# Routed rows sent in half sequences, each scatter tied to a VectorE step, five read-back slots

## The chip, the cores and the metric

One core of a Trainium2 chip runs the whole program. The metric is the time of one execution on the device, in microseconds; the median of three runs stands for a kernel. One further execution was profiled, and every row below is from it.

## What is computed

Four sequences of 11456 tokens with 128 features go through a long convolution and then, token by token, through a mixture of eight experts with top-1 routing:

```python
h_filt = (relu(pos_emb @ w1) @ w2) * exp(-0.01 * pos)[:, None]
y = irfft(rfft(x * v, n=2*S, axis=1) * rfft(h_filt, n=2*S, axis=0), axis=1)[:, :S]
x = (x * y).reshape(B * S, D)                       # B, S, D = 4, 11456, 128
logits = x @ w_gate + modality_bias[modality_id]    # 8 experts
e_idx = argmax(logits, axis=1); gate_w = softmax(logits)[e_idx]
for e in range(8):                                  # F = 1024
    out[e_idx == e] = gate_w * (relu(x @ w1[e]) @ w2[e])
```

All inputs are float32; out has 45824 rows of 128.

## The kernel before, in words

**The convolution** is written as transforms of size 90 by 64. For each sequence b there are two kinds of stage. `outer` number b works in 16 steps: it takes sequence b-1 through its inverse transform and its routing, and sequence b through its forward transform (`outer` 4 has only the first part, `outer` 1 to 3 have both). `middle` b works in 23 groups: it multiplies spectra. The order is filter, `middle` 0, `outer` 1, `middle` 1, `outer` 2, `middle` 2, `outer` 3, `middle` 3, `outer` 4, experts. A `Timeline` sorts all parts by step and by a place within the step; the engines (TensorE, VectorE, ScalarE and the SyncE queue) then keep that order. SyncE issues nearly all loads and stores, from one queue, in program order. GpSimd issues the indirect transfers.

**Routing.** Every two steps of an `outer` give one block o of 0 to 7: `choice(o)` picks an expert for 1440 rows, `store(o)` writes the rows (130 words each, with gate weight and token number) to a DRAM buffer `xr[b]`, `send(o)` counts places within each expert's region, `places(o)` writes them to `xi[b]`. When the sequence is complete, `fetch(b)`, called in group 4 of the next `middle`, loads the places (`to`). The rows come back to SBUF in pieces (`rows_back`): 128 partitions by 5 rows, in three slots, each asked for three columns before it is needed. A column is 128 rows, one to a partition, and one indirect transfer of GpSimd, here called a scatter, sends it to its places in `xs`. A sequence has 90 columns, all four have 360.

**Where scatters are issued.** `send_rows(n, behind, wait)` takes the next n columns. In `middle` it is called once a group after group 4, in GpSimd's order but without a wait for another engine. In `outer` it is called through `paced`, which makes the scatter wait for the VectorE instruction just given: two for the products of the forward transform (lines 469 and 473), one each for line 695 and line 697 of the inverse transform (three and two in `outer` 4), one for line 788 of `choice` (not for the last sequence). GpSimd's queue is in order, and a scatter also waits for the eighth before it.

**The experts** work on 82 tiles of 512 rows and up to 22 of 256. A full tile has eight steps c; each step is one block of the hidden layer (three matmuls, ScalarE's relu at line 1065, VectorE's rest at line 1066) and three matmuls of the second layer for a block two steps back. At c = 2 `rows_out` turns the tile before back (lines 1097, 1099) and issues its four output scatters at once (line 1102). The rows of the last sequence are fetched at step 18 and sent at five steps of nine, with no wait for another engine:

```python
if lo == 0 and at == FC:
    fetch(nb - 1)
if lo == 0 and 5 * at % 9 < 5:
    send_rows(1)
```

Tiles of the first 37 need the rows of the first two sequences alone (180 scatters). `rest()` makes the tables of the later tiles, one VectorE instruction a step from tile 28 (`FR = 9`).

Of the kernel before, what the change touches and what calls it, by code (L numbers as in the profile page):

```python
# [31 lines left out]
N1, N2 = 90, 64  # L32
# [38 lines left out]
FR = 9  # L71
# [20 lines left out]
def shape_constants():  # L92
# [48 lines left out]
        "c_fwd": f(fwd.reshape(D, 2 * N1)), "c_whole": f(whole.reshape(D, 2 * N1)),  # L141
        "c_inv": f(inv.reshape(N1, D)), "c_to": f(to), "c_back": f(back), "c_win": f(win.reshape(D, 2 * N2)),
# [36 lines left out]
def hyena_moe_kernel(ctx: ExitStack, tc: tile.TileContext, a: dict, out: bass.AP,  # L179
# [8 lines left out]
    NR = 4 * HALF * N2  # L188
    xr = [dram.tile([NR, RW], F32, name=f"xr{b}") for b in range(nb)]
    xi = [dram.tile([NR], I32, name=f"xi{b}") for b in range(nb)]  # L190
# [26 lines left out]
    to_t = [cst.tile([D, NR // D], I32, name=f"to{i}") for i in range(2)]  # L217
    RC = 5
    NB = NR // D // RC
    back_t = [cst.tile([D, RC, RW], F32, name=f"back{i}") for i in range(3)]  # L220
# [36 lines left out]
    def send_rows(n, behind=None, wait=None):  # L257


        for _ in range(min(n, len(waiting))):  # L260
            b, c = waiting.pop(0)
            if c % RC == 2:
                rows_back(b, c // RC + 1)
            ix, src = to_t[b % 2][:, c:c + 1], back_t[(b * NB + c // RC) % 3][:, c % RC]
# [92 lines left out]
    with ExitStack() as cv:  # L357
# [5 lines left out]
        def pair(name):  # L363
# [7 lines left out]
        win = bs2[:, 0].rearrange("p e c -> p (e c)")[:, 0:2 * N2].rearrange(  # L371
            "p (q m) -> p q m", q=NQ)
        whole = bs2[:, 2:4].rearrange("p o e c -> p (o e c)")[:, 0:2 * N1]
        wf = keepp.tile([D, 2, D], F32, name="wf")
        dve.memset(wf, 0.0)
# [41 lines left out]
        for name, of in (  # L417
                ("r", [t.rearrange("p c r -> p (c r)")[:, 0:U // 2] for t in back_t]),
                ("h0", [flat(t)[:, 0:2 * U] for t in xo_t]),
                ("seq0", [flat(t)[:, k * U:k * U + U] for t in xo_t for k in range(2)]  # L420
                 + [work[:, i * U:i * U + U] for i in range(4)])):
            ring_of[name] = [of, 0]
# [107 lines left out]
        def middle_stages(b):  # L530
# [76 lines left out]
            def spectrum(g):  # L607
# [59 lines left out]
        def inverse_stages(b):  # L667
# [57 lines left out]
        def route_stages(b):  # L725
# [36 lines left out]
            def choice(o):  # L762
# [27 lines left out]
                if b < nb - 1:  # L790
                    paced(s)

            def store(o):
                xo = xo_of(b, o)
                for blk in range(2):
                    rows = xr[b].rearrange("(k n w m) r -> k n w m r", k=2, n=HALF, w=2)
                    sp.dma_start(
                        rows[blk, :, :, 8 * o:8 * o + 8].rearrange("n w m r -> n w (m r)"),
                        xo[64 * blk:64 * blk + HALF].rearrange("p w s h r -> p w (s h r)"))

            def send(o):
# [13 lines left out]
                dve.tensor_mul(ro, ro, oh[0:PU])  # L815
# [6 lines left out]
            def places(o):  # L822
                ix = ix_t[(b * NO + o) % 2]
                for blk in range(2):
                    at = xi[b].rearrange("(k n w m) -> k n w m", k=2, n=HALF, w=2)
                    sp.dma_start(
                        at[blk, :, :, 8 * o:8 * o + 8],
                        ix[64 * blk:64 * blk + HALF].rearrange("p (w m) -> p w m", w=2))
# [57 lines left out]
        for b in range(nb + 1):  # L886
            if b:
                outer(b, at)
            if b < nb:
# [7 lines left out]
            if b == NK:  # L897
                line.put(at - 3, lambda: (dve.tensor_copy(base1, base),
                                          known.append(NK * NR // D)), 3)
# [73 lines left out]
    def experts(lo, hi):  # L973
# [4 lines left out]
        def rows_in(i):  # L978
# [11 lines left out]
            if tb == "1":  # L990

                for s in scatters[known[0]:]:
# [57 lines left out]
        def hidden(at):  # L1050
# [15 lines left out]
            dve.scalar_tensor_tensor(hl, ph, 0.0, hh.bitcast(F32), op0=ALU.max, op1=ALU.subtract)  # L1066
# [23 lines left out]
        def rows_out(i):  # L1090
# [21 lines left out]
        for at in range(len(work) + 6):  # L1112
# [19 lines left out]
            if c == 2:  # L1132
                rows_out(i - 1)

# [11 lines left out]
_INS = ["w1", "w2", "moe_w_gate", "moe_modality_bias",  # L1146
# [3 lines left out]
def device_inputs(inputs):  # L1150
# [3 lines left out]
    for name, of, lay in (("x", "x", tile4), ("xd", "x", tile8), ("v", "v", tile8)):  # L1154
# [9 lines left out]
        for a in ids])).view(np.int32).reshape(B, D, NO * NC, 2)  # L1164
    arrays.update(shape_constants())
# [18 lines left out]
```

## Time and profile before

| | us |
|---|---|
| median of 3 runs | 2283.65 (2272.26 to 2286.53) |
| the profiled execution's own time | 2303.19 |
| its span, first to last instruction | 2301.0 |
| TensorE busy in the span | 2118.4 (92%) |
| VectorE, ScalarE, GpSimd busy | 1753.4, 1317.3, 968.2 |

A matmul's end is modelled, so a busy TensorE is not one at its peak, and what a stretch costs is better read from the spacing of equal steps than from the busy share. "issue" as the releaser of a wait is time for which the profile shows no cause, "remote" an update whose sender it doesn't know. An idle engine matters only where the end waits for it.

### The profile page before, as it was taken

What the parts mean: (1) busy time and instruction counts of PE and PEld (TensorE: products, weight loads), DVE (VectorE), ACT (ScalarE), POOL (GpSimd) and SP (SyncE); (2) the same over time, 40 slices, a digit from 0 to 9 for tenths busy, and PEclk for the clock granted to TensorE, in tenths of its full rate; (3) what the DMA queues carried; (4) which work ended last, traced back from release to release, by engine and by line L of the source; (5) the groups of instructions that cost most, each with busy time, mean ns of one, the idle gap of its engine ahead of it and who ended that gap; (6) DMA issues with size and microseconds to landing.
All of it is one profiled execution on the core that took longest, in us unless ns stands there. A gap on an engine that the chain in (4) does not pass through costs nothing.

```text
span 2301.0 us, 48463 instructions
## 1 busy us (share of the span) xinstructions
PE 2118.4 (92%) x18002; PEld 1658.4 (72%) x18002; DVE 1753.4 (76%) x2790; ACT 1317.3 (57%) x2451; POOL 968.2 (42%) x910
## 2 busy tenths in 40 slices
PE   8999998989799888987788889999999999999997
PEld 7787665766477556744466667788888888888897
DVE  6677899978799779955465566778777777777796
ACT  4555674556445654444455455666666666666675
POOL 0233004855476555755234566533333333333332
PEclk9999999999899999988799899999999999999999
DMA  9354677888688887745567222111111111111110
GB/s 369 128 159 152 238 266 233 259 288 278 208 267 272 274 268 250 244 137 158 140 190 227 73 76 86 62 61 56 46 46 45 42 47 47 47 46 46 34 44 30
DMA packets 187833, 341.52 MB, mean 148 GB/s; under 512 B 31633, under 2 KB 99213, under 8 KB 187593
## 3 DMA queue, kind: packets, MB, share of 16 engines
q1 hardware_dynamic: 164137, 290.68, 39.7%
q0 software_dynamic: 23296, 47.66, 6.1%
q8 instruction: 144, 2.36, 0.4%
q14 instruction: 96, 0.79, 0.1%
q10 hardware_dynamic: 160, 0.03, 0.0%
HBM read 253.84 MB, written 84.83 MB: 147 GB/s over the span
## 4 chain that ended last, share of the span: by engine, by line
issue 41%; PE 33%; POOL 13%; DVE 6%; ACT 3%; DMA 2%; another core or an unknown queue 1%; SPq 0%; POOLq 0%; DVEq 0%; ACTq 0%
POOL out L1102 9%; PE pw L657 8%; PE pz L615 6%; PE py L690 5%; PE wt L681 4%; POOL xs L265 4%; PE s L484 3%; PE xT L738 2%; DVE work L631 1%; ACT A L487 1%; PE s L517 1%; PE pl L746 1%; PE pz L568 1%; PE pq L582 1%
## 5 line engine op out<-in xcount | busy, mean ns | idle before, releaser
L1066 DVE SCALAR_TENSOR_TENSOR hl<-ph,hh 128x512 fp32r<-128x512 f32 x724 | 497.6, 689 | 275.4 <-ACT hh L1065 167.0
L1065 ACT ACTIVATE hh<-ph 128x512 fp32r<-128x512 f32 x724 | 433.0, 600 | 412.0 <-PE ph L1062 257.3
L1102 POOL DMA_INDIRECT out<-ot,idx x362 | 355.9, 983 | 685.2 <-DVE ot L1099 600.7
L265 POOL DMA_INDIRECT xs<-back,to x360 | 388.0, 1078 | 249.9 <-issue 79.3
L1083 PE MATMUL po<-hh,wh 128*128 128x512 f32 (+1 forms) x792 | 306.4, 387 | 13.3 <-ACT hh L1065 6.7
L1060 PE MATMUL ph<-xh,wh 128*128 128x512 f32 (+1 forms) x792 | 306.7, 387 | 2.8 <-ACT wh L1031 2.2
L1085 PE MATMUL po<-hl,wh 128*128 128x512 f32 (+1 forms) x792 | 298.0, 376 | 0.1
L1062 PE MATMUL ph<-xl,wh 128*128 128x512 f32 (+1 forms) x792 | 297.8, 376 | 0.0
L1061 PE MATMUL ph<-xh,wl 128*128 128x512 f32 (+1 forms) x792 | 296.8, 375 | 0.0
L1084 PE MATMUL po<-hh,wl 128*128 128x512 f32 (+1 forms) x792 | 296.2, 374 | 0.0
L625 POOL TENSOR_TENSOR work<-work 128x512 f32<-128x512 f32 (+1 forms) x92 | 115.4, 1254 | 281.5 <-DVE work L621 281.4
L661 ACT COPY A<-pw 128x512 f32<-128x512 f32 (+1 forms) x184 | 97.0, 580 | 182.8 <-PE pw L657 182.8
L615 PE MATMUL pz<-A,work 128*64 128x256 f32 x1440 | 180.6, 393 | 6.2 <-DMA work<-in_c_to 5.7
L681 PEld LDWEIGHTS wt<-ident,A 128*90 128x90 f32 x1024 | 126.0, 185 | 79.5 <-issue 50.6
L657 PEld LDWEIGHTS pw<-work 64*128 64x128 f32 x2856 | 165.1, 188 | 25.1 <-ACT work L597 11.9
L1083 PEld LDWEIGHTS po<-hh,wh 128*128 128x128 f32 x792 | 150.5, 190 | 39.8 <-ACT hh L1065 8.6
L657 PE MATMUL pw<-work 64*128 64x128 f32 x2856 | 177.2, 277 | 0.0
L681 PE MATMUL wt<-ident,A 128*90 128x128 f32 x1024 | 148.8, 297 | 30.7 <-issue 21.6
L1085 PEld LDWEIGHTS po<-hl,wh 128*128 128x128 f32 x792 | 150.2, 190 | 32.2 <-DVE hl L1066 3.6
L1062 PEld LDWEIGHTS ph<-xl,wh 128*128 128x128 f32 x792 | 150.5, 190 | 28.2 <-DVE xl L1047 0.4
L1060 PEld LDWEIGHTS ph<-xh,wh 128*128 128x128 f32 x792 | 150.9, 191 | 26.7 <-ACT wh L1031 2.6
L682 ACT COPY work<-wt 90x512 f32<-90x512 f32 x256 | 136.7, 597 | 57.4 <-PE wt L681 25.5
(181 smaller groups left out, 3769.6 us busy)
## 6 DMA issues: line engine op xcount, KB each, us to landing
work<-hs SPq DMA_DIRECT2D x66, 512.0 KB
work<-in_x SPq DMA_DIRECT2D x64, 512.0 KB
work<-in_xd SPq DMA_DIRECT2D x54, 512.0 KB
work<-in_v SPq DMA_DIRECT2D x54, 512.0 KB
xr<-xo SPq DMA_DIRECT2D x64, 365.6 KB
back<-xr SPq DMA_DIRECT2D x72, 325.0 KB
work<-in_c_to SPq DMA_DIRECT2D x88, 256.0 KB
x<-xs SPq DMA_DIRECT2D x82, 260.0 KB
```

Source lines behind the costliest of these rows:

```text
L265: s = pool.indirect_dma_start(out=xs, out_offset=bass.IndirectOffsetOnAxis(ap=ix, axis=0), in_=src, in_offset=None, bounds_check=E * R - 1 ...
L615: pe.matmul(z[64 * s:64 * s + 64, t, r], k["b"][:, t, s, r], A[:, :, 4 * g + 2 * t + s], start=True, stop=True)
L657: pe.matmul(v[s][:, t, blk], k[of][at, t, r, blk], k["c"][at, t, r], start=i == 0, stop=i == len(terms) - 1)
L681: pe.transpose(p[0:N1, D * j:D * j + D], A[:, blk, :, 8 * q + 2 * j + c], ident)
L1060: pe.matmul(p, k[0, "h"][:, f:f + D], k["xh"], start=True, stop=False)
L1061: pe.matmul(p, k[0, "l"][:, f:f + D], k["xh"], start=False, stop=False)
L1062: pe.matmul(p, k[0, "h"][:, f:f + D], k["xl"], start=False, stop=True)
L1065: act.activation(hh, ph, AF.Relu)
L1066: dve.scalar_tensor_tensor(hl, ph, 0.0, hh.bitcast(F32), op0=ALU.max, op1=ALU.subtract)
L1083: pe.matmul(po, k[1, "h"][:, f], hh[:, t], start=g == 0, stop=False)
L1085: pe.matmul(po, k[1, "h"][:, f], hl[:, t], start=False, stop=g == NCH - 1)
L1102: s = pool.indirect_dma_start(out=out, out_offset=bass.IndirectOffsetOnAxis(ap=k["idx"][:, j:j + 1], axis=0), in_=ot[:, j, :], in_offset=N ...
```

## The change

1. `xr` and `xi` are now one buffer for each half sequence u (0 to 7, 45 columns); four `to` tiles in place of two.
2. Pieces are 3 rows to a partition in five slots (before: 5 in three), the same SBUF. `rows_back` is called ahead of every column and asks until the piece in use and two more are asked for.
3. The first half of a sequence is fetched in step 13 of its own `outer`, the second half in group 4 of the next `middle` (the last one at step 18 of the experts).
4. In `middle` one column is sent in every group. In `outer` line 697 no longer sends (it still does in `outer` 4), line 695 sends two in place of three in `outer` 4, `choice` sends in every sequence, and line 815 of `send(o)` sends one.
5. In the experts, `rows_out` only puts its four columns on a list. `pace` issues one a step at c = 3 to 6, tied to the step's line 1066, and a routed column at c = 7, 0 and 1, tied likewise. `rest()` starts at tile 32, two instructions a step.
6. At the start, `w1` and `w2` come as one array `wf` laid out by the host, by SyncE's first DMA; two tables come as one (`early`), by ScalarE's queue, ahead of its table load. GpSimd issues none of them.

```diff
-FR = 9
+FR = 5
...
-    NR = 4 * HALF * N2
-    xr = [dram.tile([NR, RW], F32, name=f"xr{b}") for b in range(nb)]
+    NR = 2 * HALF * N2
+    xr = [dram.tile([NR, RW], F32, name=f"xr{u}") for u in range(2 * nb)]
...
-    RC = 5
+    RC, NBACK = 3, 5
...
-    def rows_back(b, k):
-        if k < NB:
-            of = xr[b].rearrange("(p k c) r -> p k c r", p=D, c=RC)
-            sp.dma_start(back_t[(b * NB + k) % 3], of[:, k])
-    def fetch(b):
-        sp.dma_start(to_t[b % 2], xi[b].rearrange("(p c) -> p c", p=D))
-        rows_back(b, 0)
-        waiting.extend((b, c) for c in range(NR // D))
+    def rows_back():
+        now = waiting[0][1] // RC if waiting else len(ready)
+        while len(asked) < min(now + 3, len(ready)):
+            u, k = ready[len(asked)]
+            of = xr[u].rearrange("(p k c) r -> p k c r", p=D, c=RC)
+            sp.dma_start(back_t[len(asked) % NBACK], of[:, k])
+            asked.append((u, k))
+    def fetch(u):
+        sp.dma_start(to_t[u % 4], xi[u].rearrange("(p c) -> p c", p=D))
+        waiting.extend((u, u * NR // D + c) for c in range(NR // D))
+        ready.extend((u, k) for k in range(NB))
+        rows_back()
...
         for _ in range(min(n, len(waiting))):
-            b, c = waiting.pop(0)
-            if c % RC == 2:
-                rows_back(b, c // RC + 1)
+            rows_back()
+            u, c = waiting.pop(0)
...
         def first_constants():
+            sp.dma_start(wf, a["wf"].rearrange("p (a d) -> p a d", a=2))
+            act.dma_start(early, a["c_early"])
+            act.dma_start(fwd, a["c_fwd"].rearrange("p (c m) -> p c m", c=2))
             act.copy(warm[:, 1:2], warm[:, 0:1])
-            for j in range(2):
-                half = slice(64 * j, 64 * j + 64)
-                act.dma_start(wf[half, 1, half], a["w1"])
-            for j in range(2):
-                pool.dma_start(wf[64 * j:64 * j + 64, 0], a["w2"])
-            pool.dma_start(win, a["c_win"].rearrange("p (q m) -> p q m", q=NQ))
-            pool.dma_start(whole, a["c_whole"])
-            pool.dma_start(fwd, a["c_fwd"].rearrange("p (c m) -> p c m", c=2))
...
                 if g == GD + 2 and b > 0:
-                    fetch(b - 1)
-                if g > GD + 2:
-                    send_rows(1, s)
+                    fetch(2 * b - 1)
+                send_rows(1, s)
...
-                n = 2 if b == nb - 1 else 1
-                paced(dve.tensor_add(y[:, 0:512], py[:, 0], y[:, 512:1024]), 2 * n - 1)
+                paced(dve.tensor_add(y[:, 0:512], py[:, 0], y[:, 512:1024]), 1 + (b == nb - 1))
                 dve.tensor_sub(y[:, 512:1024], py[:, 0], y[:, 512:1024])
-                paced(dve.tensor_mul(xo_of(b, q // 2)[:, :, q % 2, :, 0:D], four(y),
-                                     four(kept.pop(q))), n)
+                s = dve.tensor_mul(xo_of(b, q // 2)[:, :, q % 2, :, 0:D], four(y),
+                                   four(kept.pop(q)))
+                if b == nb - 1:
+                    paced(s)
...
-                if b < nb - 1:
-                    paced(s)
+                paced(s)
...
-                dve.tensor_mul(ro, ro, oh[0:PU])
+                paced(dve.tensor_mul(ro, ro, oh[0:PU]))
...
             if b:
                 outer(b, at)
+                line.put(at + 13, lambda b=b: fetch(2 * b - 2), 3)
...
-            for j in range(n // D):
-                s = pool.indirect_dma_start(
-                    out=out, out_offset=bass.IndirectOffsetOnAxis(ap=k["idx"][:, j:j + 1], axis=0),
-                    in_=ot[:, j, :], in_offset=None, bounds_check=N - 1, oob_is_err=False)
-                free_rows(outs, s)
+            held.extend((k["idx"][:, j:j + 1], ot[:, j, :]) for j in range(n // D))
+
+        held, steps = [], []
+
+        def rows_away(wait=None):
+            ix, src = held.pop(0)
+            s = pool.indirect_dma_start(
+                out=out, out_offset=bass.IndirectOffsetOnAxis(ap=ix, axis=0),
+                in_=src, in_offset=None, bounds_check=N - 1, oob_is_err=False)
+            free_rows(outs, s)
+            if wait is not None:
+                tc.add_manual_dep(ins_of(s), wait.name, sync_dep, reason="pace")
+
+        def pace(i, c):
+            if held and c > 2:
+                rows_away(steps[-1])
+            elif lo == 0 and c in (7, 0, 1):
+                send_rows(1, wait=steps[-1])
...
             if lo == 0 and at == FC:
-                fetch(nb - 1)
-            if lo == 0 and 5 * at % 9 < 5:
-                send_rows(1)
+                fetch(2 * nb - 1)
+            if at < len(work):
+                pace(i, c)
             if NW1 - FR <= i < NW1:
+                next(others, 0)
                 next(others, 0)
```

The lists `ready` and `asked` hold the pieces that may be read and that have been asked for; `steps` holds every line 1066. `rows_out` of a 256-row tile, and of the last full one, issues what is left on the list at once, as before.

## Rows read from the trace of the kernel before

**Rows 1.** The page, slices of the span: GpSimd's busy tenths and TensorE's granted clock.
```profile
POOL 0233004855476555755234566533333333333332
PEclk9999999999899999988799899999999999999999
```

**Rows 2.** Windows (`outer` 1, `outer` 4, experts early and later): busy time and instructions by engine.
```profile
core 0: us, PE busy (x) PEld busy (x) DVE busy (x) ACT busy (x) POOL busy (x), PEclk, DMA share, GB/s
241.00:353.00 112.00, 106.15 (x1570) 72.13 (x1572) 103.17 (x194) 80.66 (x151) 0.00 (x0) 1.00 0.72 246
984.00:1136.00 152.00, 119.52 (x596) 70.75 (x595) 71.98 (x165) 64.00 (x122) 75.75 (x72) 0.78 0.49 136
1148.00:1479.00 331.00, 291.00 (x1284) 229.54 (x1284) 211.74 (x367) 176.99 (x324) 176.89 (x178) 0.95 0.39 125
1479.00:1800.00 321.00, 321.00 (x1517) 265.11 (x1517) 251.51 (x457) 207.98 (x380) 106.92 (x109) 1.00 0.16 50
```

**Rows 3.** Line 690 in `outer` 1 to 4: count, durations in ns, first and last start.
```profile
L690 PE MATMUL py<-work,inv x128: 592/592/832, 241.6 to 349.1; 90*64 90x512 f32 x128
L690 PE MATMUL py<-work,inv x128: 592/592/1116, 470.6 to 608.0; 90*64 90x512 f32 x128
L690 PE MATMUL py<-work,inv x128: 591/592/644, 731.4 to 862.3; 90*64 90x512 f32 x128
L690 PE MATMUL py<-work,inv x128: 592/643/1116, 984.6 to 1132.0; 90*64 90x512 f32 x128
```

**Rows 4.** Line 615 in `middle` 1 and 3, likewise.
```profile
L615 PE MATMUL pz<-A,work x360: 379/379/687, 357.8 to 461.5; 128*64 128x256 f32 x180
...
L615 PE MATMUL pz<-A,work x360: 379/379/687, 871.7 to 975.5; 128*64 128x256 f32 x180
```

**Rows 5.** Line 265, the routed scatters, around `outer` 2, in `outer` 4 and the experts.
```profile
L265 POOL DMA_INDIRECT xs<-back,to x69: 972/980/1972, 470.0 to 612.7; - x69
...
L265 POOL DMA_INDIRECT xs<-back,to x72: 977/980/1989, 988.6 to 1128.9; - x72
...
L265 POOL DMA_INDIRECT xs<-back,to x90: 977/980/1482, 1184.5 to 1469.4; - x90
```

**Rows 6.** Line 1065, one a step, in four windows of the experts.
```profile
L1065 ACT ACTIVATE hh<-ph x23: 585/598/622, 1147.9 to 1182.7; 128x512 fp32r<-128x512 f32 x23
L1065 ACT ACTIVATE hh<-ph x184: 585/598/622, 1147.9 to 1477.9; 128x512 fp32r<-128x512 f32 x184
L1065 ACT ACTIVATE hh<-ph x64: 597/598/610, 1361.6 to 1466.0; 128x512 fp32r<-128x512 f32 x64
L1065 ACT ACTIVATE hh<-ph x217: 597/598/615, 1479.3 to 1799.4; 128x512 fp32r<-128x512 f32 x109
```

**Rows 7.** GpSimd's timeline: ends of an early run, start of a later one.
```profile
1240.92 0.98 POOL L1102 DMA_INDIRECT out<-ot,idx  x1 [6.88 <-DVE ot L1099]
...
1258.90 0.98 POOL L265 DMA_INDIRECT xs<-back,to  x1 [0.30 <-issue]
...
1508.63 0.98 POOL L1102 DMA_INDIRECT out<-ot,idx  x1 [7.04 <-DVE ot L1099]
```

**Rows 8.** Waits: TensorE's loads in 1240 to 1262, ScalarE in 982 to 1140.
```profile
PEld pt L1097 <- issue: 6.6, 1, 6.6
...
ACT work L682 <- remote: 17.3, 8, 3.8
ACT work L748 <- remote: 9.0, 2, 5.1
ACT work L740 <- remote: 4.9, 4, 2.3
```

**Rows 9.** Waits: SyncE's queue for a read-back slot, GpSimd for rows.
```profile
SPq L249 <- DMA xs<-back,to: 26.8, 12, 6.0
...
POOL xs L265 <- DMA xr<-xo: 5.9, 2, 2.9
```

**Rows 10.** Timeline of the start: first loads and first matmuls.
```profile
0.76 0.88 SPq L498 DMA_DIRECT2D work<-in_pos_emb  x2
...
2.37 1.12 POOL L385 DMA_DIRECT2D wf<-in_w  x2
...
7.81 5.46 PE L504 MATMUL m<-wf,work 128*128 128x128 f32 x24 [7.81 <-DMA wf<-in_w]
```

More of the change, by code (lines that the diff above doesn't have):

```diff
@@ L140, in shape_constants @@
     return {
-        "c_fwd": f(fwd.reshape(D, 2 * N1)), "c_whole": f(whole.reshape(D, 2 * N1)),
-        "c_inv": f(inv.reshape(N1, D)), "c_to": f(to), "c_back": f(back), "c_win": f(win.reshape(D, 2 * N2)),
+        "c_fwd": f(fwd.reshape(D, 2 * N1)),
+        "c_inv": f(inv.reshape(N1, D)), "c_to": f(to), "c_back": f(back), "c_early": f(np.concatenate([win.reshape(D, 2 * N2), whole.reshape(D, 2 * N1)], 1)),
         "c_small": f(small), "c_pad": f(pad.reshape(D, -1)),
@@ L185, in hyena_moe_kernel @@
     hs = dram.tile([NM, D, 8 * D], F32, name="hs")
-    NR = 4 * HALF * N2
-    xr = [dram.tile([NR, RW], F32, name=f"xr{b}") for b in range(nb)]
-    xi = [dram.tile([NR], I32, name=f"xi{b}") for b in range(nb)]
+    NR = 2 * HALF * N2
+    xr = [dram.tile([NR, RW], F32, name=f"xr{u}") for u in range(2 * nb)]
+    xi = [dram.tile([NR], I32, name=f"xi{u}") for u in range(2 * nb)]
     xs = dram.tile([E * R + T, RW], F32, name="xs")
@@ L216, in hyena_moe_kernel @@
     ix_t = [cst.tile([D, NC], I32, name=f"ix{i}") for i in range(2)]
-    to_t = [cst.tile([D, NR // D], I32, name=f"to{i}") for i in range(2)]
-    RC = 5
+    to_t = [cst.tile([D, NR // D], I32, name=f"to{i}") for i in range(4)]
+    RC, NBACK = 3, 5
     NB = NR // D // RC
-    back_t = [cst.tile([D, RC, RW], F32, name=f"back{i}") for i in range(3)]
+    back = cst.tile([D, NBACK, RC, RW], F32, name="back")
+    back_t = [back[:, i] for i in range(NBACK)]
     oh_t = [cst.tile([D, E, NC], BF16, name=f"oh{i}") for i in range(2)]
@@ L370, in hyena_moe_kernel @@
         bs2 = keepp.tile([D, NO, E, NC], F32, name="bs2")
-        win = bs2[:, 0].rearrange("p e c -> p (e c)")[:, 0:2 * N2].rearrange(
-            "p (q m) -> p q m", q=NQ)
-        whole = bs2[:, 2:4].rearrange("p o e c -> p (o e c)")[:, 0:2 * N1]
+        early = bs2.rearrange("p o e c -> p (o e c)")[:, 0:2 * N2 + 2 * N1]
+        win = early[:, 0:2 * N2].rearrange("p (q m) -> p q m", q=NQ)
+        whole = early[:, 2 * N2:2 * N2 + 2 * N1]
         wf = keepp.tile([D, 2, D], F32, name="wf")
-        dve.memset(wf, 0.0)
         wg = keepp.tile([D, 32], F32, name="wg")
@@ L417, in hyena_moe_kernel @@
         for name, of in (
-                ("r", [t.rearrange("p c r -> p (c r)")[:, 0:U // 2] for t in back_t]),
+                ("r", [back.rearrange("p k c r -> p (k c r)")[:, i * U // 2:(i + 1) * U // 2]
+                       for i in range(3)]),
                 ("h0", [flat(t)[:, 0:2 * U] for t in xo_t]),
@@ L795, in store @@
                 for blk in range(2):
-                    rows = xr[b].rearrange("(k n w m) r -> k n w m r", k=2, n=HALF, w=2)
+                    rows = xr[2 * b + o // 4].rearrange("(k n w m) r -> k n w m r", k=2, n=HALF, w=2)
+                    m = 8 * (o % 4)
                     sp.dma_start(
-                        rows[blk, :, :, 8 * o:8 * o + 8].rearrange("n w m r -> n w (m r)"),
+                        rows[blk, :, :, m:m + 8].rearrange("n w m r -> n w (m r)"),
                         xo[64 * blk:64 * blk + HALF].rearrange("p w s h r -> p w (s h r)"))
@@ L824, in places @@
                 for blk in range(2):
-                    at = xi[b].rearrange("(k n w m) -> k n w m", k=2, n=HALF, w=2)
+                    at = xi[2 * b + o // 4].rearrange("(k n w m) -> k n w m", k=2, n=HALF, w=2)
+                    m = 8 * (o % 4)
                     sp.dma_start(
-                        at[blk, :, :, 8 * o:8 * o + 8],
+                        at[blk, :, :, m:m + 8],
                         ix[64 * blk:64 * blk + HALF].rearrange("p (w m) -> p w m", w=2))
@@ L898, in hyena_moe_kernel @@
                 line.put(at - 3, lambda: (dve.tensor_copy(base1, base),
[L899 removed]
+                                          known.append(2 * NK * NR // D)), 3)
         if NW1:
@@ L990, in rows_in @@
             if tb == "1":
+                assert len(scatters) >= known[0]
                 for s in scatters[known[0]:]:
@@ L1065, in hidden @@
             act.activation(hh, ph, AF.Relu)
-            dve.scalar_tensor_tensor(hl, ph, 0.0, hh.bitcast(F32), op0=ALU.max, op1=ALU.subtract)
+            steps.append(ins_of(dve.scalar_tensor_tensor(
+                hl, ph, 0.0, hh.bitcast(F32), op0=ALU.max, op1=ALU.subtract)))
             k["hh", c], k["hl", c] = hh, hl
@@ L1133, in experts @@
                 rows_out(i - 1)
+                while held and (i > last or tiles[i][2] != T):
+                    rows_away()
     sure = max(len(tiles) - UNSURE, 0)
@@ L1143, in hyena_moe_kernel @@
             experts(sure, len(tiles))
-_INS = ["w1", "w2", "moe_w_gate", "moe_modality_bias",
+_INS = ["moe_w_gate", "moe_modality_bias",
         "moe_w1", "moe_w2"]
@@ L1164, in device_inputs @@
         for a in ids])).view(np.int32).reshape(B, D, NO * NC, 2)
+    w1, w2 = (np.asarray(inputs[name]) for name in ("w1", "w2"))
+    wf = np.zeros((2, 64, 2, D), w1.dtype)
+    for j in range(2):
+        wf[j, :, 0], wf[j, :, 1, 64 * j:64 * j + 64] = w2, w1
+    arrays["wf"] = wf.reshape(D, 2 * D)
     arrays.update(shape_constants())
```

4 lines of the change are left out of this document (3 added, 1 removed).

## The prediction

> **What bounds the kernel now.** I read the slices of the page first: GpSimd is busy from the second tenth of the span to a little past its middle, and TensorE's granted clock is below full in the same stretch [rows 1]. So I compare stages that do the same work with and without routed scatters. `outer` 1 to 3 all run 128 of line 690 beside a forward transform. `outer` 1 has no scatter and takes 107.5 us from its first to its last; `outer` 2 and 3 take 137.4 and 130.9 [rows 3]. `outer` 4 lacks the forward transform, yet takes 147.4; there TensorE was granted 0.78 of its clock on the mean, a mixture of 2.4 and 1.2 GHz, with every engine but TensorE under half busy, where `outer` 1 has VectorE at 103 of 112 us and full clock [rows 2, 3]. `middle` 1 and 3 hold scatters too and take 103.7 and 103.8 us [rows 4]. In the experts the plain sight is the spacing of line 1065, eight a tile: later on 217 of them fill 321 us, 1.479 us a step or 11.83 a tile, with TensorE busy throughout; the first 184, 23 tiles, fill 331 us, which is 58.9 more than 23 such tiles, and the 90 scatters of the last sequence lie in just that stretch [rows 2, 5, 6].
>
> What goes with the loss is the length of a run of scatters. When nothing holds it, GpSimd starts one every 1.28 us: from 1240.92 to 1258.90 it sent fifteen in a row, and TensorE stood still for 6.6 us of it for no cause that the profile shows [rows 7, 8]. Later tiles issue four outputs and then wait 7.04 us, and TensorE loses nothing [rows 2, 7]. In `outer` 4 runs of ten occur (two steps of five), and ScalarE waited 17.3 + 9.0 + 4.9 = 31.2 us for releasers that the profile doesn't know [rows 8]. In `middle` scatters stand alone, and the stage has the same length whether it holds 19 or 23. Excess per routed scatter: (29.9 + 23.4) / 134 = 0.40 us in `outer` 2 and 3 (67 each by program order), at least 39.9 / 72 = 0.55 in `outer` 4, 58.9 / 90 = 0.65 in the experts.
>
> **The change part by part**, as a sum against the profiled execution's own 2303.19 us.
>
> **Start.** The first matmul waits for `wf` until 7.81 us; the last pieces were issued by GpSimd from 2.37 on, while SyncE issued its first load at 0.76 [rows 10]. One `wf` DMA at that place could start TensorE up to some 4 us earlier, or nothing if the large loads behind it now delay the table `early`, which the first VectorE result needs. I take 2; bounds 0 to 4.
>
> **Order of the scatters.** Counting columns in program order, `outer` 1 to 3 get 9, 57, 57 (before 0, 67, 67), `middle` 1 to 3 get 30, 30, 26 (before 22, 23, 19), `outer` 4 gets 61 (before 72), the experts 90 as before. At 0.40 us `outer` 1 to 3 save 0.40 x (134 - 123) = 4. In each pair of steps scatters tied to lines 695 and 697 (two each) become two at line 695 and one at line 815, so runs shrink little. I take 4. Bounds: minus 5, if the nine in `outer` 1, which has VectorE nearly full [rows 2], cost their 4 us and nothing is saved elsewhere; plus 20, if shorter runs take a third of the 53 away. `middle`: a scatter a group is what it carries now without loss [rows 4]; the tail of `outer` adds one a group in the first five groups, on GpSimd's queue ahead of the adds of lines 625 and 643. The cover is GpSimd's idle time there; if it fails, 5 x 1.28 us a stage. I take 0.
>
> **`outer` 4.** Five scatters a step become three, plus one in `choice` and one in `send` every second step: eight in a pair of steps in place of ten, and in place of 3 + 2 + 3 + 2 without a gap they come as three, then one, two and one, then one. By the spacing of their VectorE steps that makes runs of three and four. Such runs cost little elsewhere [rows 2, 7]. Bounds: 11 fewer x 0.55 = 6, and 40 if the stage comes down to the 107.5 of `outer` 1. I take 25, nearer to the upper end, since ScalarE's unexplained waits alone are 31.2 [rows 8], and the clock would rise again once TensorE stands still less.
>
> **Experts.** A tile now issues seven scatters, one a step at c = 3 to 6 (output) and 7, 0, 1 (routed), none at c = 2, each behind its line 1066. At 1.48 us a step on the mean they needn't run at 1.28. Ninety columns at three a tile last 30 tiles in place of 22. What is left of the 58.9: before the first routed scatter at 1184.5, the 22 steps up to 1182.7 took 34.8 us against 32.5 [rows 5, 6], so 2.3 is not theirs; for the routing that the experts finish in tiles 0 to 2 and for weight loads I leave 8 in all, an estimate. The 30 tiles cost between nothing, as with four in a row [rows 2, 7], and what tiles with eight or nine in a row cost: 64 steps from 1361.6 to 1466.0 are 11.2 us longer than 63 x 1.479, 1.4 a tile, 42 in 30 tiles [rows 6]. I take 0.3 a tile, 9, near the lower end, because the routed part falls from 4.4 to 3 and no two are closer than a step. So 58.9 - 17 = 42 is saved; bounds 9 and 57. Behind a waiting scatter on GpSimd's queue stand only other scatters; an output leaves up to five steps later, and its tile has seven buffers.
>
> **Read-backs and SyncE's queue.** 72 reads become 120; behind each on SyncE's queue stand the loads of the stage. A read waits for its slot: 26.8 us in 12 waits before, with seven columns between the slot's last scatter and the read, now six [rows 9]. The loads behind it are issued one to five steps ahead of use, which hides a wait of 2.2 us; without that cover, 19 reads in an `outer` at 2.2 us would be 42. GpSimd itself waited only 5.9 us for rows. `fetch` in step 13 waits for `places(3)`, issued a step earlier; the later halves wait as `fetch` did. I take 0.
> Against this stands a rule of the Trainium skill, "DMA: Bandwidth & Descriptors", section "Rules for kernel authors": merge small transfers; its section on the anatomy of one DMA gives each a fixed cost of about 2 us. By an estimate from that figure 48 more reads would add 96 us if they were on the path, and the sum would be 2326 for a profiled execution; GpSimd's 5.9 us of waiting speaks against that [rows 9].
>
> **`rest()`** puts two small VectorE instructions into a step of five tiles where VectorE is 78% busy [rows 2]: 0, at most 1 us.
>
> **How the numbers follow.** 2 + 4 + 25 + 42 = 73 us, so 2230 for a profiled execution. That is 19.5 us above the median of the runs. If the difference scales, 73 / 2303.19 of the median is 72, giving 2211; if all of it is stall (152 us of excess named above, 132.5 outside the profile), 64, giving 2220. I predict 2217. All upper bounds together save 121 (2163), all lower ones 10 (2274).
>
> **Rivals.**
> *Runs survive.* GpSimd lags, scatters tied to a past step run at 1.28 us all the same, and seven in a row act like eight. For it: a step is only 0.20 us longer than a scatter's 1.28. Against it: the idle step in each tile, and the longest run falls from fifteen to seven. It leaves 2 + 4 + 6 + 9 = 21 saved: 2263.
> *The stalls are not the scatters'.* ScalarE's unknown waits come from elsewhere and only coincide. Against it: `outer` 1, `middle` and the later tiles [rows 2 to 4]. Only the start is saved: 2281. The Trainium skill, "SBUF — State Buffer", section "Who interferes with whom", says that TensorE and ScalarE never wait on others for SBUF. By that rule spacing scatters would win nothing on those two engines; the waits of ScalarE beside the runs speak against it [rows 8].
> *The tie itself costs (slower).* Scatters with a wait for VectorE, in `outer` 2 and 3, cost 0.40 us each; those without, in `middle`, nothing; and the outputs of the later tiles, untied now, cost nothing. Tied in 82 tiles, 328 outputs at 0.40 are 131 us against the 67 saved: 2283.65 - 67 + 131 = 2348. It decides from 67 / 328 = 0.2 us a scatter. Against it: the experts' routed scatters are untied and cost most; VectorE is nearly full in `outer`, and not in the experts [rows 2].
>
> **Chances.** Forecast 0.62 (its own range 2185 to 2250), runs survive 0.20, not the scatters' 0.07, tie 0.08, other 0.03. About 1% is what a measurement can tell from no change: 2261 to 2306. Runs survive falls half on either side of 2261, so faster 0.73, same 0.18, slower 0.09. The range, 2180 to 2267, takes in the forecast and runs survive and leaves the rest out.
>
> **What the changed profile would show.** Line 1065 of tiles 3 to 22 at 12.0 to 12.4 us a tile, with the last routed scatter near tile 29; line 690 of `outer` 4 spanning about 120 us with a granted clock over 0.85, and ScalarE's unknown waits there near 5 us; `outer` 2 and 3 within 5 us of before; `middle` unchanged; the first matmul before 7 us. Wrong would be: the first tiles still at 13 us and more, later tiles above 11.9 (the tie), or SyncE's waits for slots well above 27 us with loads late.

## Result and profile after

| | before | changed |
|---|---|---|
| median of 4 runs, us | 2285.09 (2272.26 to 2291.19) | 2187.76 (2179.16 to 2190.84) |
| profiled execution, own time (span) | 2303.19 (2301.0) | 2187.52 (2185.7) |

The ratio is 0.9575, 95% interval [0.9526, 0.9624]: 97 us faster. **It holds for the chip of these runs and not in general.** On four other chips the kernel before took 2145 to 2146 us, and the changed one, run on one of the four, took 2147; on a fifth, before took 2288 us again. Most of what follows is about that. Each chip was met in one set of runs, so "chip" stands here for the chip and for whatever else it was doing at that time. The record doesn't number the chip of the first runs, so that the fifth is another one is not shown.

The page of the changed kernel, slices as in [rows 1], and the chain that ended last by engine. TensorE's granted clock is under 0.9 in two slices in place of five, and the chain is now TensorE for the most part. (Before, 41% of it was "issue"; but that counts some 6.8 us in each of the later tiles too, which lose nothing, and is no measure of what was lost.)

```profile
POOL 0133003775568555865555666633333333333332
PEclk9999998999999999999899999999999999999999
...
PE 78%; DVE 8%; issue 6%; ACT 3%; DMA 2%; POOL 1%; SPq 1%; another core or an unknown queue 0%; DVEq 0%; POOLq 0%; ACTq 0%
```

Line 691 of the changed kernel (690 before) in `outer` 1 to 4, as [rows 3]: 119.1, 118.0, 117.5 and 99.9 us, against 107.5, 137.4, 130.9 and 147.4. `outer` 1, which has scatters now, became longer by 11.6, the others shorter by 19.4, 13.4 and 47.5.

```profile
L691 PE MATMUL py<-work,inv x128: 592/592/1115, 238.2 to 357.3; 90*64 90x512 f32 x128
L691 PE MATMUL py<-work,inv x128: 592/592/644, 483.8 to 601.8; 90*64 90x512 f32 x128
L691 PE MATMUL py<-work,inv x128: 592/592/644, 726.0 to 843.5; 90*64 90x512 f32 x128
L691 PE MATMUL py<-work,inv x128: 592/592/1117, 965.3 to 1065.2; 90*64 90x512 f32 x128
```

The experts' first 184 steps (line 1070, as [rows 6]) and their routed scatters (as [rows 5]):

```profile
L1070 ACT ACTIVATE hh<-ph x184: 587/598/621, 1083.1 to 1362.2; 128x512 fp32r<-128x512 f32 x184
...
L272 POOL DMA_INDIRECT xs<-back,to x90: 971/1024/1191, 1088.0 to 1434.8; - x90
```

The window of `outer` 4, as [rows 2], with a granted clock of 0.96:

```profile
965.00:1067.00 102.00, 92.94 (x579) 55.56 (x577) 68.62 (x162) 60.23 (x119) 60.76 (x56) 0.96 0.65 183
```

Waits: what ScalarE still waited for an unknown releaser from 965 to 1083, as [rows 8].

```profile
ACT work L683 <- remote: 3.8, 1, 3.8
```

Timeline: the first matmul, as [rows 10].

```profile
4.99 1.41 PE L506 MATMUL m<-wf,work 128*128 128x128 f32 x5 [4.99 <-DMA work<-in_pos_emb]
```

The 184 steps take 279.1 us from first to last start, against 330.0.

### The profile page after: what moved, and what is told of

Its sections match the earlier page's. It is cut to its first block, busy times and chain, and to the rows that moved or that the text cites. A ratio compares the mean times of both kernels' runs of the same rounds, so it can differ in the third digit from the quotient of the medians.

```text
span 2185.7 us, 48874 instructions
## 1 busy us (share of the span) xinstructions
PE 2072.5 (95%) x18002; PEld 1632.5 (75%) x18002; DVE 1755.0 (80%) x2789; ACT 1314.2 (60%) x2451; POOL 979.8 (45%) x905
## 4 chain that ended last, share of the span: by engine, by line
PE 78%; DVE 8%; issue 6%; ACT 3%; DMA 2%; POOL 1%; SPq 1%; another core or an unknown queue 0%; DVEq 0%; POOLq 0%; ACTq 0%
PE pw L658 8%; PE ph L1067 7%; PE ph L1065 7%; PE ph L1066 7%; PE po L1091 7%; PE po L1089 7%; PE po L1090 7%; PE pz L617 6%; PE py L691 5%; PE wt L682 4%; PE s L486 3%; PE xT L740 2%; PE pt L1103 2%; PE px L1048 2%; PE pl L748 1%
## 5 line engine op out<-in xcount | busy, mean ns | idle before, releaser
L1113 POOL DMA_INDIRECT out<-ot,idx x362 | 368.4, 1018 | 578.5 <-DVE hl L1071 427.6
L1066 PEld LDWEIGHTS ph<-xh,wl 128*128 128x128 f32 x792 | 150.1, 190 | 24.4 <-DVE wl L1037 0.4
L1090 PEld LDWEIGHTS po<-hh,wl 128*128 128x128 f32 x792 | 149.9, 189 | 23.3
L691 PE MATMUL py<-work,inv 90*64 90x512 f32 x512 | 139.2, 623 | 17.3 <-issue 6.5
```

Of the source, the lines that this page charges most:

```text
L1066: pe.matmul(p, k[0, "l"][:, f:f + D], k["xh"], start=False, stop=False)
L1090: pe.matmul(po, k[1, "l"][:, f], hh[:, t], start=False, stop=False)
L1113: s = pool.indirect_dma_start(out=out, out_offset=bass.IndirectOffsetOnAxis(ap=ix, axis=0), in_=src, in_offset=None, bounds_check=N - 1, o ...
```

## Experiments: the parts, one at a time

Four kernels on one chip: the experts' spacing alone on the kernel before, the changed kernel without it, the slots alone, and the changed kernel with the old places in `outer`.

Experts' spacing alone, added to before:

```diff
+            held.extend((k["idx"][:, j:j + 1], ot[:, j, :]) for j in range(n // D))
+            if held and c > 2:
+                rows_away(steps[-1])
+            elif lo == 0 and c in (7, 0, 1):
+                send_rows(1, wait=steps[-1])
-            if lo == 0 and 5 * at % 9 < 5:
-                send_rows(1)
```

> The kernel before with the experts' part of the change alone: outputs held and issued one a step at c = 3 to 6, routed columns at c = 7, 0 and 1, each tied to its line 1066 (rest starts at tile 33). Whole sequences, three slots of five rows and the places in outer as before. Theory 1 (long runs of scatters stall the other engines): nearly all of the experts' share goes, about 48 us, so about 2237 and a ratio of 0.979, with tiles 3 to 22 near 11.9 us. Theory 2 (the gain comes from reading back earlier in smaller pieces, and the runs only follow from late rows): within 10 us of before, ratio 0.996 to 1.004.

The changed kernel with these lines as before:

> The changed kernel with the experts' issue as before: four outputs at once at c = 2, routed columns at five steps of nine with no wait. Half sequences, five slots and the new places in outer stay. Theory 1: the experts' loss comes back, about 45 us over the changed kernel, so about 2233 and a ratio of 0.977, with tiles at 13 us and more as long as routed columns last. Theory 2: as the changed kernel, about 2190, ratio 0.958.

Slots alone, `RC, NBACK = 3, 5` and the new `rows_back` on before, whole sequences kept:

> The kernel before with five slots of three rows, read two pieces ahead, alone; whole sequences and all places of scatters as before. Theory 1: runs are as long as before or longer, since rows wait for them less; 2275 to 2295, ratio 0.995 to 1.004. Theory 2: half of the gain or more, 2235 or less, ratio under 0.98.

The changed kernel with before's places in `outer`:

```diff
-            paced(dve.tensor_add(y[:, 0:512], py[:, 0], y[:, 512:1024]), 1 + (b == nb - 1))
+            paced(dve.tensor_add(y[:, 0:512], py[:, 0], y[:, 512:1024]), 2 * n - 1)
...
-                paced(dve.tensor_mul(ro, ro, oh[0:PU]))
+                dve.tensor_mul(ro, ro, oh[0:PU])
```

> The changed kernel with the places in outer as before (line 697 sends, lines 695 and 697 send three and two in outer 4, no send at line 815, none in choice of the last sequence); half sequences, five slots and the experts' part stay. Theory 1: outer 4 gets its runs of ten back and most of its 47 us, outer 2 and 3 some of their 33; about 50 over the changed kernel, 2238, ratio 0.979. Theory 2: as the changed kernel, about 2190, ratio 0.958.

| | us | ratio to before |
|---|---|---|
| before, on this chip | 2145.99 (2140.96 to 2152.42, 30 runs) | |
| spacing alone | 2152.43 | 1.0027 [1.0016, 1.0037] |
| changed without it | 2145.88 | 1.0000 [0.9988, 1.0012] |
| slots alone | 2154.24 | 1.0035 [1.0021, 1.0050] |
| changed, old places in `outer` | 2144.65 | 0.9988 [0.9977, 0.9999] |

The times of all four expectations missed, since here the kernel before itself ran 139 us shorter than in the first runs. By the ratio, the spacing alone came out as theory 2 has it and the slots alone as theory 1; the other two fit neither. With nothing to win here, the four say nothing between the theories. What the slots alone lose lies in `outer` 2 and 3: line 698 (690 before), as [rows 3], spans 115.8 and 111.8 us there, against 108.5 in each of them in before on the next chip.

```profile
L698 PE MATMUL py<-work,inv x128: 592/593/1114, 469.5 to 585.3; 90*64 90x512 f32 x128
L698 PE MATMUL py<-work,inv x128: 592/593/644, 707.4 to 819.2; 90*64 90x512 f32 x128
```

## Experiments: the same two kernels on another chip

> The changed kernel itself, in a new set of runs. Why: four variants on one chip all came out within 0.4% of the kernel before, which itself took 2146 us there and not 2285 us. Theory A (the stall belongs to the chip: beside a long run of scatters TensorE and ScalarE are held up on one chip and not on another; the change takes away what the stall feeds on, and nothing else): where the kernel before takes about 2146 us, the changed one takes 2140 to 2160 us, ratio 0.997 to 1.006; where it takes about 2285 us, 2188 us, ratio 0.957. Theory B (the halves and the two pacings are worth some 4% only together, on any chip): ratio 0.955 to 0.965 wherever it runs, so about 2055 us where before takes 2146 us.

> A copy of the kernel before, for its trace on this chip; its time against the kernel before is 1.000 within 0.3%. Where it takes about 2146 us, theory A expects the same runs of back-to-back scatters as in the first trace (the longest 15, three of 8 or more in outer 4) with TensorE's idle gaps under 1 us beside them, outer 4's line 690 in 100 us or less against 147.4 us, and the experts' first 23 tiles in 274 to 280 us against 331 us. Theory C (the runs themselves fall apart there: GpSimd issues the scatters later or faster, so the two engines are not held): runs shorter than 8 or starts well under 1.28 us apart.

And the changed kernel with the experts' routed columns in bursts:

```diff
-            elif lo == 0 and c in (7, 0, 1):
-                send_rows(1, wait=steps[-1])
+            elif lo == 0 and c == 7 and i % 3 == 2:
+                send_rows(9, wait=steps[-1])
```

> The changed kernel with the experts' routed columns issued nine at once at the end of every third tile, after one VectorE step, in place of three a tile each after a step of its own: about the same number of scatters, in about ten runs of nine. Theory A, where the kernel before takes about 2285 us: each run of nine costs what tile 1 of the changed kernel lost beside its one run of nine (18.16 against 12.04 us), so 30 to 60 us slower than the changed kernel, 2215 to 2250 us; where it takes about 2146 us: within 0.4% of the changed kernel. Rival (the spacing inside the experts is worth nothing anywhere; what the change gained it gained by the halves in the outer groups): within 0.4% of the changed kernel on either kind of chip.

Before 2146.14 us (25 runs), the copy of it 2146.67, the changed kernel 2147.32, ratio 1.0010 [0.9995, 1.0025], the bursts 2146.35, 1.0002 [0.9990, 1.0014]. Theory B falls: the changed kernel is worth nothing here. The bursts decide nothing, since both their theories gave the same for such a chip.

The trace of the copy of before on this chip: line 690 in the four `outer`, then the 184 steps.

```profile
L690 PE MATMUL py<-work,inv x128: 592/592/916, 242.3 to 349.9; 90*64 90x512 f32 x128
L690 PE MATMUL py<-work,inv x128: 592/592/643, 472.0 to 580.5; 90*64 90x512 f32 x128
L690 PE MATMUL py<-work,inv x128: 592/592/644, 701.5 to 810.0; 90*64 90x512 f32 x128
L690 PE MATMUL py<-work,inv x128: 592/592/797, 930.4 to 1024.1; 90*64 90x512 f32 x128
...
L1065 ACT ACTIVATE hh<-ph x184: 588/598/613, 1047.4 to 1320.6; 128x512 fp32r<-128x512 f32 x184
```

107.6, 108.5, 108.5 and 93.7 us, and 273.2: every stage that the first trace showed stretched is close to its plain length. The scatters were not gentler here but denser. From 1126.05 on GpSimd sent 99 in a row, 1.31 us apart on the mean and never more than 1.58, the last at 1254.42; by that measure the longest run in the first trace was fifteen. GpSimd's groups from 1126 to 1255 (count, busy time, mean ns, idle time before them):

```profile
L265 POOL DMA_INDIRECT xs<-back,to x55 | 55.7, 1013 | 16.8 <-issue 16.1 <-DMA x<-xs 0.3 <-DMA xs<-back,to 0.3
L1102 POOL DMA_INDIRECT out<-ot,idx x44 | 43.8, 995 | 19.3 <-issue 9.4 <-DVE ot L1099 6.2 <-DMA out<-ot,idx 2.1
```

ScalarE's waits there:

```profile
ACT hh L1065 <- PE ph L1062: 45.0, 75, 0.8
```

The engines' busy time in the window, as [rows 2]:

```profile
1126.00:1254.00 128.00, 128.00 (x605) 105.67 (x604) 97.70 (x162) 82.80 (x152) 98.40 (x98) 1.00 0.35 110
```

TensorE is busy for 128.00 of 128 us; ScalarE waits for a matmul 0.8 us at most. So theory C falls too, and with it the idea that a long run of scatters by itself holds TensorE up by what the first chip showed.

What differs is how late a finished matmul is seen. The same pair on each chip, the third matmul of a hidden block and the relu that needs it: first before on the first chip, with the matmul of the second layer that waits for the relu,

```profile
1184.99 0.39 PE L1062 MATMUL ph<-xl,wh 128*128 128x512 f32 x1
...
1190.90 0.60 ACT L1065 ACTIVATE hh<-ph 128x512 fp32r<-128x512 f32 x1 [5.12 <-remote]
...
1191.55 0.80 PE L1083 MATMUL po<-hh,wh 128*128 128x512 f32 x1 [3.46 <-ACT hh L1065]
```

then the copy on the later chip:

```profile
1131.83 0.39 PE L1062 MATMUL ph<-xl,wh 128*128 128x512 f32 x1
...
1132.26 0.60 ACT L1065 ACTIVATE hh<-ph 128x512 fp32r<-128x512 f32 x1 [0.76 <-PE ph L1062]
```

The relu starts 0.04 us after the matmul's end here and 5.52 us after it there. (TensorE ran on for two more blocks meanwhile, until it needed this relu; the next two relus of that trace start at 1195.14 and 1197.07.) ScalarE had nothing else to do, and the semaphore that the relu waits for (the counter by which TensorE tells ScalarE that it is done) was updated at 1190.84 by the trace's own record: it is the signal that is late. Both pairs lie inside a run of scatters 1.28 us apart.

The packed traces differ in one more thing, in the later tiles too, where nothing is lost. Of the semaphore updates that DMA engines make, the trace of before holds 14950 on the first chip and 24853 on this one, for the same program; the changed kernel's hold 17178 and 25541. So a wait's releaser is less sure on the first chip: SyncE's waits for a read-back slot in before, 26.8 us in 12 by the first trace [rows 9], are 108.7 in 41 here, and 36.6 in 17 in the changed kernel. The stalls themselves don't rest on such names, since the spacing of equal steps shows them.

```profile
SPq L249 <- DMA xs<-back,to: 108.7, 41, 8.6
...
SPq L254 <- DMA xs<-back,to: 36.6, 17, 5.2
```

The changed kernel on this chip, lines as above:

```profile
L691 PE MATMUL py<-work,inv x128: 592/592/1117, 239.6 to 347.5; 90*64 90x512 f32 x128
L691 PE MATMUL py<-work,inv x128: 592/592/645, 470.5 to 579.4; 90*64 90x512 f32 x128
L691 PE MATMUL py<-work,inv x128: 592/592/643, 701.2 to 809.6; 90*64 90x512 f32 x128
L691 PE MATMUL py<-work,inv x128: 592/592/644, 930.9 to 1021.7; 90*64 90x512 f32 x128
...
L1070 ACT ACTIVATE hh<-ph x184: 588/598/613, 1043.7 to 1315.9; 128x512 fp32r<-128x512 f32 x184
```

107.9, 108.9, 108.4, 90.8 and 272.2 us. Beside these the changed kernel on the first chip still carried 11.2 + 9.1 + 9.1 + 9.1 us of stall in the `outer` stages and 6.9 in the experts, 45 in all; before carried -0.1 + 28.9 + 22.4 + 53.7 and 56.8, 162 in all. The change took away 116 us of stall that exists on one kind of chip.

A little of it is elsewhere too. With the old places `outer` 4 spans 92.4 to 98.8 us in the six traces of them on chips without the stall, with the new ones 90.6 to 90.8 in five: the old places cost some 2 to 8 us there. What waits for what in them was not looked into, and on the whole the change wins nothing on the chip of this section.

Two of the parts on a third chip, where before took 2146.46 us:

> The changed kernel with the experts' scatters issued as before the change (four at a time, unpaced), in a new set of runs, to find the change's parts where the stall is. Theory A, where the kernel before takes about 2285 us: the outer groups keep their gain and the experts lose theirs (the first 23 tiles took 280.4 against 331.3 us), so about 2188 + 45 = 2233 us, ratio 0.97 to 0.985. Rival there (the halves and the outer groups' spacing set how many scatters are still left for the experts, and that is what counted): 2190 to 2205 us. Where the kernel before takes about 2146 us: within 0.4% of it by both, as before.

> The kernel before with the experts' pacing alone, in a new set of runs. Theory A, where the kernel before takes about 2285 us: the experts gain what the change gained there, some 40 to 50 us, and the outer groups nothing: 2235 to 2250 us. Rival there (with whole sequences and the outer groups as before, more scatters are left for the experts, and the pacing gains little): 2270 to 2290 us. Where the kernel before takes about 2146 us: 2146 to 2156 us by both.

2147.08 us, 1.0001 [0.9989, 1.0014], and 2151.32 us, 1.0033 [1.0015, 1.0050]: as on the first of these chips. The kernel with the spacing alone is thus 5 to 6 us longer where there is no stall, but not by the spacing: its first 184 steps take 272.2 us. It starts the tables of the later tiles at tile 33, one tile later than the change does, and loses 6.4 us in tiles 34 and 35, where the changed kernel loses some 1.5 in tiles 33 and 35. From 1455 to 1482 TensorE waits for VectorE there:

```profile
L1065 ACT ACTIVATE hh<-ph x184: 587/598/615, 1047.3 to 1319.5; 128x512 fp32r<-128x512 f32 x184
...
PEld po L1086 <- DVE hl L1066: 4.7, 2, 4.2
```

## Experiments: is it other traffic?

```diff
+    junk = [dram.tile([6, D, F], F32, name=f"junk{k}") for k in range(4)]
...
+            if lo == 0 and i < 24 and c == 6:
+                act.dma_start(junk[i % 4], a["moe_w1"][0:6])
```

> The kernel before with 3 MB more of copies from DRAM to DRAM in each of the experts' first 24 tiles, issued by ScalarE on a queue of its own: the kernel's own work is unchanged. It asks whether a busy DMA side can bring out, beside the runs of scatters, the late releases that the first trace of the kernel before showed (ScalarE and TensorE waiting 3 to 6 us with nothing in their way) and the three later chips did not. Theory D (the stall is contention of long scatter runs with other transfers, wherever those come from): the experts' first 184 steps go from 274 us to 290 to 340 us, with waits of ScalarE and TensorE put down to issue or remote of over 2 us beside runs of 8 or more. Rival E (traffic of the core's own does not do it): 274 to 285 us for these steps, what is added being waits that end on a transfer; the source of the stall stays open. A copy of 3 MB takes about 7.5 us at the 400 GB/s that the first slices show, so there is room for it in a tile of 11.85 us.

> The changed kernel with the same copies in the same 24 tiles. Theory D: at most a third of the loss of the kernel before with copies, since no run of scatters is longer than 5 there but the one at the start; so 275 to 295 us for the first 184 steps. Rival E: the same as the kernel before with copies, within 5 us.

Before took 2144.93 us on this chip; with the copies 2214.72 us, 1.0327 [1.0290, 1.0363], and the changed kernel with them 2190.30 us, 1.0213 [1.0181, 1.0244] (two runs each). The first 184 steps took 342.6 and 317.3 us. The former is just above what theory D gave and far above rival E's, the latter lies between the two, so neither held in its numbers. In both kernels the first seven tiles lose the most (122.0 and 123.6 us, against 84.9 in the copy of before without copies), mostly in waits that start with weights: the room that the expectation counted on was not there. From the eighth on, before with copies, line 1066 up to the 184th step:

```profile
L1066 ACT ACTIVATE hh<-ph x128: 597/598/613, 1173.2 to 1392.5; 128x512 fp32r<-128x512 f32 x128
```

Waits of TensorE from 1190 to 1394 and of SyncE's queue from 1170:

```profile
PE px L1044 <- DMA x<-xs: 16.6, 7, 3.5
...
SPq L250 <- DMA xs<-back,to: 178.0, 16, 20.7
```

And SyncE's timeline:

```profile
1237.47 0.33 SPq L250 DMA_DIRECT2D back<-xr  x1
1238.37 0.34 SPq L990 DMA_DIRECT2D x<-xs  x1
1251.89 0.33 SPq L250 DMA_DIRECT2D back<-xr  x1
1252.79 0.34 SPq L990 DMA_DIRECT2D x<-xs  x1
```

The changed kernel with copies, likewise (the view lists no wait of TensorE's from 1190 to 1367):

```profile
L1071 ACT ACTIVATE hh<-ph x128: 597/598/615, 1173.7 to 1366.1; 128x512 fp32r<-128x512 f32 x128
```

```profile
SPq L255 <- DMA xs<-back,to: 36.9, 12, 5.0
```

```profile
1236.03 0.33 SPq L255 DMA_DIRECT2D back<-xr  x1
1242.39 0.34 SPq L994 DMA_DIRECT2D x<-xs  x1
```

No wait in either trace is "remote", and TensorE's in this window all end on a transfer. That is rival E's mechanism with far more time than it gave: busy DMA engines of the core's own did not bring the first chip's stall out on this one. What they bring out is another queue. In before, SyncE stands 178 us for a slot that scatters still hold, and the read of sorted rows behind it goes out 0.9 us after each read-back, too late for TensorE, which waits 16.6 us for such rows. In the changed kernel the read is not bound to the read-back: it goes out 6.4 us after it here, and TensorE doesn't wait for it. So 128 steps take 219.3 us from first to last against 192.4: 27 us, where the two kernels' times are 24 apart.

Which part does that, slots or spacing?

> The changed kernel with the experts' scatters issued as before the change (not spaced), and the same copies in 24 tiles. With the copies the kernel before took 342.6 us for the experts' first 184 steps and the changed one 317.3 us; in the former SyncE waited 178 us in 16 waits for a read-back slot that scatters still held, and each read of sorted rows was issued 0.9 us behind such a read-back. Theory F (the half sequences and five slots give SyncE room): 315 to 325 us for these steps and 2188 to 2198 us. Theory G (the spacing does it: unspaced scatters leave slots and rows late whatever the slots): 335 to 345 us and 2206 to 2218 us.

It ran on none of the four chips so far, and there before took 2287.87 us (2261.09 to 2309.01, 9 runs): the first kind. The kernel with copies took 2262.56 us, outside what either theory gave for the other kind, so F and G stay undecided. But up to the experts its program is that of the changed kernel, and line 692 shows these stages in a second set of runs with the stall; below it the steps from the eighth tile on:

```profile
L692 PE MATMUL py<-work,inv x128: 592/592/1115, 240.2 to 354.7; 90*64 90x512 f32 x128
L692 PE MATMUL py<-work,inv x128: 592/592/645, 481.4 to 599.6; 90*64 90x512 f32 x128
L692 PE MATMUL py<-work,inv x128: 592/592/643, 723.5 to 838.8; 90*64 90x512 f32 x128
L692 PE MATMUL py<-work,inv x128: 592/592/1116, 962.5 to 1062.8; 90*64 90x512 f32 x128
...
L1071 ACT ACTIVATE hh<-ph x129: 593/598/631, 1212.6 to 1432.7; 128x512 fp32r<-128x512 f32 x129
```

ScalarE's waits from 1240 to 1375:

```profile
ACT hh L1071 <- remote: 8.8, 6, 3.1
```

114.5, 118.2, 115.3 and 100.3 us, within 5 of the changed kernel on the first chip; the experts begin at 1082.7 (1083.1 there, and 1147.9 in before there; before itself was not profiled in this second set). In the experts, unspaced and with the copies, 129 steps take 220.1 us and "remote" is back. This trace, too, holds few semaphore updates by DMA engines: 16547, where the same program without copies has 25652 on a chip without the stall.

## Why the prediction came out

The time lay in the range, 8 us above its lower end, and the sum, 73 us on the profiled execution, was 43 short of the 115.7 measured there: every large term was too small. That it came out at all is in part luck. The loss that it set out to remove was met in two sets of runs and is missing on four other chips; on the one of these where the change itself ran, it is worth nothing.

- **The order of reading was right.** The excess that it read off, by comparing stages that do the same work, is what the later chips show: 29.9 and 23.4 us in `outer` 2 and 3 against 28.9 and 22.4, and 58.9 in the experts against 56.8.
- **`outer` 4, 25 us with a bound of 40: 47.5.** The mis-sized step is the bound, "if the stage comes down to the 107.5 of `outer` 1". This stage has no forward transform, and its plain length is 93.7. The profile was to show about 120 us, a clock over 0.85 and near 5 us of ScalarE's unknown waits; it shows 99.9, 0.96 and 3.8.
- **`outer` 1 to 3, 4 us: 21.2.** A price of 0.40 us a scatter was the wrong form. `outer` 1 became 11.6 us longer; about 3 of that came at its start, where no scatter is near, and some 8 beside six scatters at its end. `outer` 2 gained 19.4 with 57 scatters in place of 67. "`outer` 2 and 3 within 5 us of before" was wrong.
- **Experts, 42 us: 50.9.** From the third tile on, 167 spacings fill the 248.9 us from 1113.3 to 1362.2, 1.490 us each where the plain step is 1.482 (320.1 us over 216 spacings [rows 6]; the prediction's 1.479 divides by 217): under 0.1 us a tile, where 0.3 was left to them, and tiles 3 to 22 take 11.9 us where 12.0 to 12.4 were expected. The last routed scatter, at 1434.8, came in tile 29, as said.
- **Start, 2 us: 2.8** at the first matmul. **`middle` and the read-backs, 0:** the four gains make 122.4 us, and 6.7 of them were lost again in what the sum put at nothing. From the last of `outer` 1 to the first of `outer` 2 it takes 126.5 us in place of 121.5, and from the last of `outer` 4 to the experts 17.9 in place of 15.9. The former hold the tail of `outer` 1 and `middle` 1, with 30 columns in place of 22 by the prediction's count; whether those or the reads cost it was not tried. On the chip without the stall it is 123.0 against 122.1, and the changed kernel is within 0.25% of before: the 48 more reads can cost little there. The Trainium skill's "DMA: Bandwidth & Descriptors", section "Rules for kernel authors", would merge them; no run here shows the 96 us that the prediction made of its figure, which the page gives for transfers that GpSimd issues, and these are SyncE's.
- **Runs survive** falls: it left 9 us of gain to the experts and 6 to `outer` 4. **The tie** falls on the first chip; elsewhere the kernel with the spacing alone costs 0.3% through VectorE's table work, not through waits for ties.
- **The stalls are not the scatters'** was given 0.07 and falls as it stands, since far more than the start was saved; but it has a true side. On the chips without the stall unspaced scatters delay TensorE and ScalarE by little (128.00 of 128 us busy beside 99 of them), and there the Trainium skill's rule ("SBUF — State Buffer", section "Who interferes with whom") that TensorE and ScalarE wait for no one over SBUF agrees with the trace. On the other kind they do wait, for a late signal, of which that rule doesn't speak, and the change takes most of it away. So the step that failed is "what goes with the loss is the length of a run of scatters", taken as the cause. It is right as a correlation on the first chip; but elsewhere longer runs cost some 2 to 8 us in `outer` 4 and about nothing in the experts, so something else of the chip must come to it, which no row of the kernel before could show.

What that is stays open. Shown are the late signals, their place beside scatters, and that traffic of the core's own did not make them on a chip without the stall. Traffic of others on the same chip was not tried; that the times of before spread by 19 and 48 us in the two sets with the stall and by 5 to 12 on the four other chips would fit something that changes from run to run. On a stalling chip the change is shown to be worth its time as a whole. Ahead of the experts that is halves, slots, places and start together, with before profiled on the first chip alone; no single part, the experts' spacing included, was measured by itself there, since the kernels that would split them met only chips without the stall.

## What to carry to other kernels

A time without a cause in the trace ("issue", "remote") may belong to the chip and not to the kernel: before tuning against it, run the kernel before on another chip. The change as a whole cost at most 0.25% on a chip without the stall and won 4% on one with it, so it is worth having where a program may meet either. With busy DMA engines, reads that waited for a buffer held the loads queued behind them on SyncE's queue (178 us in 16 waits); give such a ring slack.

## What was not expected of the hardware

One program, no input changed, takes 2145 to 2146 us on four chips, and 2285 and 2288 in two sets of runs on others. Its matmuls (592 ns for line 690), its scatters (0.98 us each, 0.30 us apart) and its steady tiles (11.85 us) are the same on both kinds; what differs is that, beside scatters, a matmul's end reaches ScalarE late, by 5.5 us in the pair shown, and that the trace holds a third to two fifths fewer semaphore updates by DMA engines. Copies of 3 MB a tile, against that, cost 70 us on a chip without the stall, in waits that mostly start with a transfer.
